# Stages two and three of a three-layer kernel in token groups of 460 and 464 columns; last stores, two sums and first keys issued from other engines

## The chip, the cores and the metric

The kernel runs on one core of one Trainium2 chip. A time is the device time of one execution in microseconds (us). Before the change it was 1575.15 us, the median of three runs (1574.21 to 1580.14).

## The reference, cut to what matters

```python
def _attn_ref(q, k, v):                       # 8 batches, 8 heads, 576 positions, 64 wide
    q_s = softmax(q, axis=-1)                 # over the 64 of a head
    k_s = softmax(k, axis=2)                  # over the 576 positions
    kv = np.einsum('bhsd,bhse->bhde', k_s, v)
    return np.einsum('bhsd,bhde->bhse', q_s, kv)

x = attn_out.transpose(0, 2, 1, 3).reshape(4608, 512)
g = np.maximum(x @ w_in1, 0.0) ** 2           # 512 -> 2048
y = g @ w_out1                                # 2048 -> 512
h = y @ w_in2                                 # 512 -> 2048
out = (h / (1 + np.exp(-h))) @ w_out2         # 2048 -> 512, fp32 result of 4608 x 512
```

## The kernel before, in words

There are four stages. Stage one computes the attention for nine blocks of 512 tokens (`i` from 0 to 8) and, for each block, `x @ w_in1` with relu and square. Its matmuls write `h`, ScalarE turns them into the tile `gs`, and for each of eight channel pairs `j` four sums of quarters follow: two on VectorE (`g_first`), two on GpSimd (`g_second`). Then GpSimd issues the store of seven pieces to the DRAM tensor `g1d` (`g_store`).

The three later matmuls, `@ w_out1` (stage two, `ph == 1` in the code), `@ w_in2` with silu (stage three, `ph == 2`) and `@ w_out2` (last stage, `ph == 3`), each use a two by two scheme with seven products in place of eight. Tokens are split in two halves, so 2304 columns stand for 4608 tokens. Each stage takes these columns in five groups `u`, of 448, 448, 448, 448 and 512. A group has 56 steps, a step six matmuls: two output or input halves times three, since each fp32 operand is split in a rounded part (`ah`, `wh`) and a rest (`al`, `wl`) and the product rest by rest is left out. So one group of one stage is 336 matmuls, every one with a weight tile of its own of 128 columns.

For each step SP loads a piece of 128 rows by the group's columns into `al` (14 steps ahead), ScalarE copies it rounded to `ah`, and VectorE subtracts to leave the rest in `al` (six steps ahead). Results come out of the PSUM banks `x`, `d` and `a` into slots of the tile `st`, and GpSimd issues their stores to `x2d` (after stage two) and `g2d` (after stage three). The last stage transposes on VectorE (`turn`) and stores to `out` (`store`); for the last group the stores are shared out over GpSimd, SP and ScalarE, 16 for each half of the result. While a stage runs, the weights of the next are made ready: sums `wt` on GpSimd, splits `wB`, `wT`, `wN` on ScalarE and VectorE. From block 1 on each engine executes in the order in which the code is written; only the first block is ordered by a scheduler. DMAs issued from SP and ScalarE share eight completion semaphores in turn, so each waits until the one eight before it has landed. In the first block `r_load` loads the last 64 positions of the keys, `kr`, with GpSimd as the issuing engine.

Of the kernel before, what the change touches and what calls it, by code (L numbers as in the profile page):

```python
# [8 lines left out]
F32 = mybir.dt.float32  # L9
# [4 lines left out]
ALU = mybir.AluOpType  # L14
# [11 lines left out]
def kernel(  # L26
# [56 lines left out]
    P = 128  # L83
# [5 lines left out]
    HB = TB // 2  # L89
    NB = NT // TB  # L90
    KC = DM // P
    NF = DFF // P
    NG = NF // 2
# [40 lines left out]
    def back(*ts):  # L134
# [8 lines left out]

    GROUPS = NB * HB // (2 * Q)
    NS = -(-NB // 2)
    sizes = [GROUPS // NS + (u >= NS - GROUPS % NS) for u in range(NS)]
    starts = [sum(sizes[:u]) * 2 * Q for u in range(NS + 1)]
    x2d = [dpool.tile([P, 7, NB * HB], F32, name=f"x2d{e}") for e in range(2)]
    g2d = [
        [dpool.tile([P, 7, n * 2 * Q], F32, name=f"g2d{u}_{j}") for j in range(NG)]  # L150
        for u, n in enumerate(sizes)
    ]
    g1d = [dpool.tile([P, 7, NB * HB], F32, name=f"g1d{j}") for j in range(NG)]
    wd = {(ph, f): dpool.tile([P, DM], F32, name=f"wd{ph}_{f}") for ph in (1, 2, 3) for f in range(NF)}

# [589 lines left out]

    def g_second(i, j):
        t = g_place(i, j)
        gp.tensor_tensor(t[:, S2], t[:, S1], t[:, A11], op=ALU.subtract)
        gp.tensor_tensor(t[:, S4], t[:, A12], t[:, S2], op=ALU.subtract)

    def g_store(i, j):
        o = slice(A21, 7) if i == 0 else slice(0, A21 + 1) if i is None else slice(0, 7)
# [73 lines left out]
    steps += [(3, u, n, j, u == ORDER3[-1]) for u in ORDER3 for n, j in SUMMED]  # L826
    xs = {}

    def width(u):
        return sizes[u] * 2 * Q  # L830

    def a_load(ph, u, n, c):

        lo = room(F32R, "al")
        slot = PRODUCTS[n][0]
        w = width(u)
        cols = slice(starts[u], starts[u + 1])
        if ph == 1:
            src = g1d[c][:, slot, cols]
        else:  # L840
            src = x2d[c][:, slot, cols] if ph == 2 else g2d[u][c][:, slot]
        sp.dma_start(out=f32(lo)[:, 0:w], in_=src)
        xs[ph, u, n, c] = [None, lo]

    def a_split(ph, u, n, c):
        hi = room(F32R, "ah")
        lo = xs[ph, u, n, c][1]
        o = slice(0, width(u))
        ac.copy(hi[:, o], f32(lo)[:, o])
        ve.tensor_tensor(lo[:, o], f32(lo)[:, o], f32(hi)[:, o], op=ALU.subtract)  # L850
        xs[ph, u, n, c][0] = hi
# [22 lines left out]

    def step(ph, u, n, j, done):
        name, begins = INTO[n]
        w = width(u)
        now = due()
        if ph == 2:
            k = j % 2  # L880
            if begins:
                ps[name, k] = bank(name)
            for c in range(2):
                hi, lo = xs[ph, u, n, c]
                mm3(
                    ps[name, k][:, 0:w], begins and c == 0, c == 1, W[ph, j, n],
                    slice(c * P, (c + 1) * P), hi[:, 0:w], lo[:, 0:w], not begins,
                )
                if j == NG - 1:
                    back(hi, lo)  # L890
                    del xs[ph, u, n, c]
            for fn in now:
                fn()
            hidden_after(ph, u, n, k, j)
        else:
            hi, lo = xs.pop((ph, u, n, j))
            for e in range(2):
                if begins and j == 0:
                    ps[name, e] = bank(name)
                mm3(  # L900
                    ps[name, e][:, 0:w], begins and j == 0, j == NG - 1, W[ph, j, n],
                    slice(e * P, (e + 1) * P), hi[:, 0:w], lo[:, 0:w], not begins,
                )
            back(hi, lo)
            for fn in now:
                fn()
            if j == NG - 1:
                for e in range(2):
                    if ph == 1:
                        hidden_after(ph, u, n, e, e)  # L910
                    else:
                        out_after(u, n, e, done)
        if done:
            back(W.pop((ph, j, n)))
# [2 lines left out]

    def hidden_after(ph, u, n, k, j):

        w = width(u)  # L920
        to = g2d[u][j] if ph == 2 else x2d[j][:, :, starts[u]:starts[u + 1]]

        def silu(x):
            if ph == 2:
                ac.activation(x, x, AF.Silu)
        p = ps[INTO[n][0], k][:, 0:w]
        h = keep.setdefault(k, {})

        def new(*names):
            for x in names:  # L930
                h[x] = slots.popleft()

        def store(*which):
            for s, x in which:
                gp.dma_start(out=to[:, s], in_=h[x][:, 0:w])
                slots.append(h.pop(x))

        at_ = lambda x: h[x][:, 0:w]

        if n == 0:  # L940
            new("c11")
            ac.copy(at_("c11"), p)
        elif n == 2:
            new("c12")
            ac.copy(at_("c12"), p)
        elif n == 4:
            ve.tensor_tensor(at_("c11"), p, at_("c11"), op=ALU.add)
            back(ps.pop(("a", k)))
        elif n == 1:
            new("c22")  # L950
            ac.copy(at_("c22"), p)
            d = ps["d", k][:, 0:w]

            def then():
                ve.tensor_tensor(at_("c22"), d, at_("c22"), op=ALU.add)
                later(lambda: silu(at_("c22")), 2)
            later(then)
        elif n == 5:
            new("c21", "s1", "s2")
            if ph == 2:  # L960
                ac.activation(at_("c21"), p, AF.Silu)
            else:
                ac.copy(at_("c21"), p)
            back(ps.pop(("x", k)))
            silu(at_("c11"))

            def then():
                ve.tensor_tensor(at_("s1"), at_("c21"), at_("c22"), op=ALU.add)
                ve.tensor_tensor(at_("c21"), at_("c11"), at_("c21"), op=ALU.subtract)
                ve.tensor_tensor(at_("s2"), at_("s1"), at_("c11"), op=ALU.subtract)  # L970
                store((A22, "c22"), (S1, "s1"), (S3, "c21"), (A11, "c11"))
            later(then)
        elif n == 6:
            ve.tensor_tensor(at_("c12"), p, at_("c12"), op=ALU.add)
            back(ps.pop(("d", k)))
            mine = keep.pop(k)

            def then():
                a12, s2 = (mine[x][:, 0:w] for x in ("c12", "s2"))
                silu(a12)  # L980

                def last():
                    s4 = slots.popleft()
                    ve.tensor_tensor(s4[:, 0:w], a12, s2, op=ALU.subtract)
                    for s, t in ((S2, mine["s2"]), (A12, mine["c12"]), (S4, s4)):
                        gp.dma_start(out=to[:, s], in_=t[:, 0:w])
                        slots.append(t)
                later(last)
            later(then, 3)

    def out_after(u, n, e, done):

        w = width(u)
        p = ps[INTO[n][0], e][:, 0:w]
        p0, u2, u3 = (st[e][:, s, 0:w] for s in (4, 5, 6))
        if n == 0:
            ac.copy(p0, p)
        elif n == 2:
            ac.copy(u2, p)
        elif n == 4:  # L1000
            ve.tensor_tensor(p0, p, p0, op=ALU.add)
            back(ps.pop(("a", e)))
            turn(u, 1, e, p0)
        elif n == 1:
            ac.copy(u3, p)
            d = ps["d", e][:, 0:w]

            def then():
                ve.tensor_tensor(u3, d, u3, op=ALU.add)
                turn(u, 0, 2 + e, u3)  # L1010
            later(then)
        elif n == 6:
            ve.tensor_tensor(u2, p, u2, op=ALU.add)
            back(ps.pop(("d", e)))
            turn(u, 1, 2 + e, u2)
            if e == 1:
                store(u, 1, done)
        elif n == 5:
            turn(u, 0, e, p)
            back(ps.pop(("x", e)))  # L1020
            if e == 1:
                store(u, 0, done)

    def turn(u, half, e, x):

        w = width(u)
        t = st[half][:, 0:4].rearrange("p n c -> p (n c)")[:, 0:4 * w]
        ve.transpose(
            t.rearrange("p (b e i) -> p e b i", e=4, i=Q)[:, e],
            x.rearrange("p (b i) -> p b i", i=Q),  # L1030
        )

    def store(u, half, ends):
        w = width(u)
        t = st[half][:, 0:4].rearrange("p n c -> p (n c)")[:, 0:4 * w]
        n = 2 * Q
        for i in range(NB):
            m0, m1 = (max(0, min(w, i * HB + x - starts[u])) // n for x in (0, HB))
            if m0 == m1:
# [15 lines left out]
            for j, nj, o in os:  # L1055
                for a in range(P // Q):
                    for r in range(2):
                        (gp if not ends or (a, r) in ((0, 0), (2, 1)) else ac if r else sp).dma_start(
                            out=o[a, half, r],
                            in_=t[a * Q + j:a * Q + j + nj].rearrange(  # L1060
                                "j (m r f) -> r j m f", r=2, f=P
# [25 lines left out]

    warm = [spool.tile([P, 1], F32, name=f"warm{x}") for x in range(3)]
    kv_load(0, 0, ac)
    r_load(0, 0, gp, ac)  # L1090
    ve.memset(warm[0], 0.0)
    ve.memset(warm[2], 0.0)
    gp.partition_all_reduce(warm[1], warm[0], P, bass_isa.ReduceOp.max)
# [187 lines left out]
```

## Time and profile before

| | us |
|---|---|
| median of three runs | 1575.15 |
| profiled execution, device time | 1569.96 |
| its span, first to last instruction | 1568.1 |
| TensorE busy in it | 1527.3 (97%) |
| VectorE, ScalarE, GpSimd busy | 1125.8, 907.0, 625.2 |

In the profile PE is TensorE's matmul, PEld its weight load, DVE VectorE, ACT ScalarE, POOL GpSimd, SP the engine that only issues DMAs; a q behind a name is that engine's sequencer, which issues DMAs and handles semaphores. All instructions of the kernel's body pass through one helper and have line L73, so they are told apart by the names of their tiles. Stage one lasts until about 500 us, stage two to 854, stage three to 1204, the last stage to 1554. A busy PE is not yet a PE at its peak.

### The profile page before, as it was taken

The numbers are of one execution on the slowest core, as the hardware profiler recorded it, in microseconds if no ns is written. First come the engines' busy times: TensorE is split into PE (matmuls) and PEld (weight loads), VectorE is DVE, ScalarE is ACT, GpSimd is POOL, SyncE is SP. The second block draws the span as 40 slices with busy tenths as digits, with TensorE's granted clock in tenths as the row PEclk, the third lists the DMA queues.
The fourth block names the chain that finished last, engine by engine and source line by source line (L and its number), as shares of the span: only waits on it lengthen the run. The fifth ranks groups of instructions, "written<-read, shape, count | busy, mean of one in ns | idle before, by whom it ended". The sixth has DMA issues, their size and how long they took to land.

```text
span 1568.1 us, 25313 instructions
## 1 busy us (share of the span) xinstructions
PE 1527.3 (97%) x7679; PEld 1329.8 (85%) x7679; DVE 1125.8 (72%) x2263; ACT 907.0 (58%) x1927; POOL 625.2 (40%) x966
## 2 busy tenths in 40 slices
PE   5899999999999999999999999999999999999996
PEld 3678888888888899999988999999888899889995
DVE  7887888986627977767888776767757865564644
ACT  7876666666545755554575664555646744454431
POOL 1035556655659020211144544445485040605231
PEclk9999999999999999999999999999999999999998
DMA  8969999999977898989996776877889777868761
GB/s 216 287 204 286 310 326 312 328 328 298 333 242 240 292 309 271 331 274 328 304 318 224 245 285 245 297 272 261 310 290 315 235 237 200 247 182 240 207 228 47
DMA packets 270376, 419.58 MB, mean 268 GB/s; under 512 B 70272, under 2 KB 202496, under 8 KB 270240
## 3 DMA queue, kind: packets, MB, share of 16 engines
q1 hardware_dynamic: 216912, 246.39, 51.9%
q0 software_dynamic: 50976, 170.50, 30.0%
q10 hardware_dynamic: 2352, 1.08, 0.3%
q8 instruction: 60, 0.98, 0.3%
q14 instruction: 76, 0.62, 0.1%
HBM read 236.72 MB, written 181.14 MB: 266 GB/s over the span
## 4 chain that ended last, share of the span: by engine, by line
PE 91%; DVE 3%; DMA 2%; ACT 2%; issue 1%; POOL 1%; SPq 0%; POOLq 0%; ACTq 0%; DVEq 0%
PE x L73 37%; PE h L73 23%; PE d L73 19%; PE a L73 9%; PE kvps L73 2%; PE xps L73 2%; DVE wu L73 1%; ACT gs L73 0%; DMA al<-g2d 0%; DMA kr<-in_k_dram 0%; DMA wraw<-in_moe_w_in_dram 0%; DVE al L73 0%; DVE xr L73 0%; DMA g1d<-gs 0%; DMA g2d<-st 0%
## 5 line engine op out<-in xcount | busy, mean ns | idle before, releaser
L73 DVE TENSOR_TENSOR al<-al,ah 128x448 fp32r<-128x448 f32 (+1 forms) x630 | 374.6, 644 | 181.4 <-ACT ah L73 179.2
L73 ACT CAST ah<-al 128x448 fp32r<-128x448 f32 (+1 forms) x630 | 334.6, 577 | 143.6 <-PE x L73 54.1
L73 PE MATMUL h<-x,wh 128*128 128x512 f32 x1152 | 364.3, 396 | 1.3 <-ACT wh L73 0.7
L73 PE MATMUL x<-ah,wT 128*128 128x448 f32 (+1 forms) x960 | 287.3, 370 | 0.0
L73 PEld LDWEIGHTS h<-x,wh 128*128 128x128 f32 x1152 | 214.5, 189 | 47.2 <-ACT wh L73 1.2
L73 ACT COPY st<-x 128x448 f32<-128x448 f32 (+1 forms) x181 | 98.1, 543 | 248.5 <-PE x L73 237.2
L73 PE MATMUL h<-x,wl 128*128 128x512 f32 x576 | 225.9, 392 | 0.0
L73 PEld LDWEIGHTS x<-ah,wT 128*128 128x128 f32 x960 | 180.3, 188 | 19.8 <-ACT st L73 0.7
L73 POOL DMA_DIRECT2D out_dram<-st x184 | 96.6, 535 | 243.5 <-DVE st L73 237.0
L73 POOL DMA_DIRECT2D g2d<-st x262 | 140.8, 542 | 130.4 <-ACT st L73 64.1
L73 PE MATMUL x<-al,wT 128*128 128x448 f32 (+1 forms) x480 | 177.6, 370 | 0.0
L73 POOL TENSOR_TENSOR gs<-gs 128x256 f32<-128x256 f32 x144 | 124.2, 865 | 106.4 <-DVE gs L73 50.9
L73 ACT ACTIVATE gs<-h 128x512 f32<-128x512 f32 x144 | 86.0, 597 | 136.6 <-PE h L73 129.3
L73 PE MATMUL a<-ah,wB 128*128 128x448 f32 (+1 forms) x480 | 148.4, 370 | 0.0
L73 PE MATMUL x<-ah,wB 128*128 128x448 f32 (+1 forms) x480 | 144.7, 373 | 0.0
L73 PE MATMUL d<-ah,wB 128*128 128x448 f32 (+1 forms) x480 | 143.6, 370 | 0.0
L73 PE MATMUL d<-ah,wT 128*128 128x448 f32 (+1 forms) x480 | 143.5, 370 | 0.0
L73 PE MATMUL x<-ah,wN 128*128 128x448 f32 (+1 forms) x480 | 143.5, 370 | 0.0
L73 PEld LDWEIGHTS h<-x,wl 128*128 128x128 f32 x576 | 108.6, 189 | 23.6 <-issue 0.5
L73 DVE TENSOR_TENSOR st<-st 128x448 f32<-128x448 f32 (+1 forms) x161 | 100.0, 647 | 25.9 <-ACT st L73 21.0
L73 DVE TENSOR_TENSOR gs<-gs 128x256 f32<-128x256 f32 x144 | 74.9, 525 | 41.3 <-ACT gs L73 24.0
L73 PEld LDWEIGHTS x<-ah,wB 128*128 128x128 f32 x480 | 90.9, 189 | 9.7
(130 smaller groups left out, 2689.5 us busy)
## 6 DMA issues: line engine op xcount, KB each, us to landing
g1d<-gs POOLq DMA_DIRECT2D x64, 896.0 KB, 6.6
al<-g1d SPq DMA_DIRECT2D x224, 224.0 KB, 4.2
al<-g2d SPq DMA_DIRECT2D x224, 224.0 KB, 3.3
g2d<-st POOLq DMA_DIRECT2D x210, 224.0 KB, 3.7
al<-g1d SPq DMA_DIRECT2D x56, 256.0 KB, 4.2
al<-g2d SPq DMA_DIRECT2D x56, 256.0 KB, 3.1
g2d<-st POOLq DMA_DIRECT2D x52, 256.0 KB, 3.7
al<-x2d SPq DMA_DIRECT2D x56, 224.0 KB, 5.1
```

Of the source, the lines that this page charges most:

```text
L73: got = fn(*a, **kw)
```

## The change

Stages two and three take their 2304 columns in groups of 460, 460, 460, 460 and 464; the last stage keeps 448 and 512. Since the groups of stage three and of the last stage no longer agree, `g2d` becomes one tensor per `j` over all columns, as `g1d` and `x2d` already are. For the last block of stage one `g_second` is issued on VectorE in place of GpSimd. The 16 stores of each half of the last group are issued on SP and ScalarE alone, eight each. The first block's `kr` is loaded from SP in place of GpSimd, as SP's first two DMAs.

```diff
-    sizes = [GROUPS // NS + (u >= NS - GROUPS % NS) for u in range(NS)]
-    starts = [sum(sizes[:u]) * 2 * Q for u in range(NS + 1)]
+    sizes = [(GROUPS // NS + (u >= NS - GROUPS % NS)) * 2 * Q for u in range(NS)]
+    even = [NB * HB // NS // 4 * 4] * (NS - 1)
+    even.append(NB * HB - sum(even))
+    SIZES = {1: even, 2: even, 3: sizes}
+    STARTS = {ph: [sum(x[:u]) for u in range(NS + 1)] for ph, x in SIZES.items()}
-    g2d = [
-        [dpool.tile([P, 7, n * 2 * Q], F32, name=f"g2d{u}_{j}") for j in range(NG)]
-        for u, n in enumerate(sizes)
-    ]
+    g2d = [dpool.tile([P, 7, NB * HB], F32, name=f"g2d{j}") for j in range(NG)]
...
     def g_second(i, j):
         t = g_place(i, j)
-        gp.tensor_tensor(t[:, S2], t[:, S1], t[:, A11], op=ALU.subtract)
-        gp.tensor_tensor(t[:, S4], t[:, A12], t[:, S2], op=ALU.subtract)
+        by = ve if i == NB - 1 else gp
+        by.tensor_tensor(t[:, S2], t[:, S1], t[:, A11], op=ALU.subtract)
+        by.tensor_tensor(t[:, S4], t[:, A12], t[:, S2], op=ALU.subtract)
...
-                        (gp if not ends or (a, r) in ((0, 0), (2, 1)) else ac if r else sp).dma_start(
+                        (gp if not ends else ac if r else sp).dma_start(
...
-    r_load(0, 0, gp, ac)
+    r_load(0, 0, sp, ac)
```

Two places where instructions move. The first is the end of stage one. On GpSimd before the change, the sums `gs` stand between the stores of `g1d` for j = 1 to 4:

```order
L73 DMA g1d1_128<-gs_186 896x1x256
L73 TENSOR_TENSOR gs_187<-gs_187 128x256 x2
L73 DMA g1d2_129<-gs_187 896x1x256
L73 TENSOR_TENSOR gs_187<-gs_187 128x256 x2
L73 DMA g1d3_130<-gs_187 896x1x256
L73 TENSOR_TENSOR gs_188<-gs_188 128x256 x2
L73 DMA g1d4_131<-gs_188 896x1x256
```

GpSimd after the change, from the last weight sums `wt` to the store of j = 6:

```order
L73 TENSOR_TENSOR wt_5181<-wB21_5174,wt_5181 128x256
L73 TENSOR_TENSOR wt_5190<-wB21_5183,wt_5190 128x256
L73 DMA g1d1_96<-gs_154 896x1x256
L73 DMA g1d2_97<-gs_155 896x1x256
L73 DMA g1d3_98<-gs_155 896x1x256
L73 DMA g1d4_99<-gs_156 896x1x256
L73 DMA g1d5_100<-gs_156 896x1x256
L73 DMA g1d6_101<-gs_154 896x1x256
```

Only stores are left there. VectorE in the same place before the change, from two splits `wB` of weights to the splits `wT` for the second product (`al` is a split of stage two's first group):

```order
L73 TENSOR_TENSOR wB11_5214<-wB11_5214 128x256
L73 TENSOR_TENSOR gs_187<-gs_187 128x256 x2
L73 TENSOR_TENSOR gs_188<-gs_188 128x256 x4
L73 TENSOR_TENSOR al_5352<-al_5352,ah_5440 128x448
L73 TENSOR_TENSOR al_5354<-al_5354,ah_5445 128x448
L73 TENSOR_TENSOR al_5373<-al_5373,ah_5467 128x448
L73 TENSOR_TENSOR al_5375<-al_5375,ah_5472 128x448
L73 TENSOR_TENSOR gs_186<-gs_186 128x256 x2
L73 TENSOR_TENSOR al_5395<-al_5395,ah_5495 128x448
L73 TENSOR_TENSOR al_5397<-al_5397,ah_5500 128x448
```

VectorE after the change, the same stretch:

```order
L73 TENSOR_TENSOR wB11_5182<-wB11_5182 128x256
L73 TENSOR_TENSOR gs_155<-gs_155 128x256 x6
L73 TENSOR_TENSOR gs_156<-gs_156 128x256 x6
L73 TENSOR_TENSOR al_5320<-al_5320,ah_5408 128x460
L73 TENSOR_TENSOR al_5322<-al_5322,ah_5413 128x460
L73 TENSOR_TENSOR gs_156<-gs_156 128x256 x2
L73 TENSOR_TENSOR al_5341<-al_5341,ah_5435 128x460
L73 TENSOR_TENSOR al_5343<-al_5343,ah_5440 128x460
L73 TENSOR_TENSOR gs_154<-gs_154 128x256 x2
L73 TENSOR_TENSOR al_5363<-al_5363,ah_5463 128x460
L73 TENSOR_TENSOR al_5365<-al_5365,ah_5468 128x460
```

There are 16 sums `gs` in place of 8 in this stretch; the splits keep their order. The second place is the end of the program on ScalarE, before the change: the stores of one half of the last group, the last two splits, the stores of the other half.

```order
L73 CAST ah_16167<-al_16085 128x448
L73 DMA out_0_dram<-st_5530 32x3x128 x3
L73 DMA out_0_dram<-st_5530 32x4x128 x3
L73 CAST ah_16196<-al_16100 128x448
L73 CAST ah_16205<-al_16111 128x448
L73 DMA out_0_dram<-st_5529 32x3x128 x3
L73 DMA out_0_dram<-st_5529 32x4x128 x3
```

The same on ScalarE after the change:

```order
L73 CAST ah_16135<-al_16053 128x448
L73 DMA out_0_dram<-st_5498 32x3x128 x4
L73 DMA out_0_dram<-st_5498 32x4x128 x4
L73 CAST ah_16164<-al_16068 128x448
L73 CAST ah_16173<-al_16079 128x448
L73 DMA out_0_dram<-st_5497 32x3x128 x4
L73 DMA out_0_dram<-st_5497 32x4x128 x4
```

Eight stores stand where six stood, ahead of the last two splits too. SP changes in the same way, and GpSimd's last instruction becomes a store of the group before the last.

## Rows read from the trace of the kernel before

**Rows 1.** Busy time by stretch (us; then PE, PEld, DVE, ACT, POOL; clock, DMA share, GB/s).
```profile
512.00:515.00 3.00, 3.00 (x9) 2.63 (x8) 3.00 (x9) 2.22 (x7) 0.90 (x1) 0.50 0.97 300
642.00:710.00 68.00, 68.00 (x337) 63.02 (x336) 51.12 (x107) 36.32 (x77) 10.62 (x21) 1.00 0.91 305
778.00:854.00 76.00, 76.00 (x337) 62.92 (x336) 66.75 (x113) 50.55 (x107) 31.96 (x34) 1.00 0.87 292
1128.00:1204.00 76.00, 76.00 (x337) 62.92 (x336) 48.34 (x77) 40.17 (x80) 54.26 (x90) 1.00 0.88 308
1204.00:1220.00 16.00, 15.14 (x73) 12.84 (x72) 15.96 (x36) 13.89 (x38) 6.92 (x13) 1.00 0.88 313
```

**Rows 2.** Chain that ended last: start us, us, what; a 448 and a 512 group.
```profile
525.21 9.72 PE x L73 x48
789.03 10.88 PE d L73 x48
```

**Rows 3.** Groups of instructions by form: busy us, mean ns of one, idle before.
```profile
L73 PEld LDWEIGHTS x<-ah,wT 128*128 128x128 f32 x960 | 180.3, 188 | 19.8 <-ACT st L73 0.7
L73 DVE TENSOR_TENSOR al<-al,ah 128x448 fp32r<-128x448 f32 x504 | 291.9, 627 | 149.3 <-ACT ah L73 147.9 <-DMA al<-g2d 1.2
```

**Rows 4.** Timeline (start us, us, what), TensorE in a 448 and a 512 group (loads, a matmul).
```profile
620.10 0.39 PEld L73 LDWEIGHTS a<-ah,wB 128*128 128x128 f32 x2
620.30 0.57 PE L73 MATMUL a<-ah,wB 128*128 128x448 f32 x2
...
799.98 0.41 PEld L73 LDWEIGHTS x<-ah,wT 128*128 128x128 f32 x2
```

**Rows 5.** Timeline of TensorE at half clock: two matmuls, two others between them.
```profile
513.53 0.57 PE L73 MATMUL x<-al,wB 128*128 128x448 f32 x1
...
514.65 0.57 PE L73 MATMUL x<-al,wB 128*128 128x448 f32 x1
```

**Rows 6.** Timeline around the end of stage one, five engines.
```profile
452.88 0.89 DVE L73 TENSOR_TENSOR gs<-gs 128x256 f32<-128x256 f32 x2 [2.88 <-ACT gs L73]
...
468.95 14.04 POOL L73 TENSOR_TENSOR wt<-wB,wt 128x256 f32<-128x256 f32 x18
...
487.34 3.90 DVE L73 TENSOR_TENSOR wB<-wB 128x256 fp32r<-128x256 f32 x2 [11.22 <-POOL wt L73]
...
495.21 1.78 POOL L73 TENSOR_TENSOR gs<-gs 128x256 f32<-128x256 f32 x2
...
503.17 0.63 ACT L73 ACTIVATE gs<-gs 128x512 f32<-128x512 f32 x1
...
509.58 1.78 DVE L73 TENSOR_TENSOR al<-al,ah 128x448 fp32r<-128x448 f32 x1
...
511.42 0.47 PE L73 MATMUL x<-al,wB 128*128 128x448 f32 x1 [3.53 <-DVE al L73]
```

**Rows 7.** Closing line L1276, engine op xcount: ns min/median/max, first and last start.
```profile
L1276 POOLq EVENT_SEMAPHORE  x4: 17/17/17, 1567.4 to 1568.0; - x4
L1276 POOLq DRAIN  x3: 46/102/10698, 1556.7 to 1567.9; - x3
```

**Rows 8.** Timeline of the last 20 us, issues of stores and ScalarE's last splits.
```profile
1549.76 1.03 ACT L73 CAST ah<-al 128x448 fp32r<-128x448 f32 x2 [13.59 <-DMA out_dram<-st]
1555.03 3.12 ACTq L73 DMA_DIRECT2D out_dram<-st  x6
...
1555.29 2.18 POOL L73 DMA_DIRECT2D out_dram<-st  x4 [6.30 <-DVE st L73]
```

**Rows 9.** DMA issues after 1554 us: xcount, KB each, median us to landing.
```profile
out_dram<-st SPq DMA_DIRECT2D x3, 64.0 KB, 3.2
out_dram<-st ACTq DMA_DIRECT2D x3, 48.0 KB, 2.4
```

**Rows 10.** Timeline of the first 10 us: the first keys `kr` and their user.
```profile
1.28 1.38 POOL L73 DMA_DIRECT2D kr<-in_k_dram  x2 [0.83 <-POOLq L1264]
...
9.12 0.29 DVE L73 TENSOR_TENSOR m<-m,kr 128x128 f32<-128x128 f32 x1 [0.77 <-DMA kr<-in_k_dram]
```

More of the change, by code (lines that the diff above doesn't have):

```diff
@@ L827, with width, columns @@
     xs = {}
-    def width(u):
-        return sizes[u] * 2 * Q
+    def width(ph, u):
+        return SIZES[ph][u]
+    def columns(ph, u):
+        return slice(*STARTS[ph][u:u + 2])
     def a_load(ph, u, n, c):
@@ L835, in a_load @@
         slot = PRODUCTS[n][0]
[L836 to L841, printed above, removed]
+        w = width(ph, u)
+        src = (g1d, x2d, g2d)[ph - 1][c][:, slot, columns(ph, u)]
         sp.dma_start(out=f32(lo)[:, 0:w], in_=src)
@@ L847, in a_split @@
         lo = xs[ph, u, n, c][1]
-        o = slice(0, width(u))
+        o = slice(0, width(ph, u))
         ac.copy(hi[:, o], f32(lo)[:, o])
@@ L876, in step @@
         name, begins = INTO[n]
-        w = width(u)
+        w = width(ph, u)
         now = due()
@@ L918, in hidden_after @@
     def hidden_after(ph, u, n, k, j):
-        w = width(u)
-        to = g2d[u][j] if ph == 2 else x2d[j][:, :, starts[u]:starts[u + 1]]
+        w = width(ph, u)
+        to = (g2d if ph == 2 else x2d)[j][:, :, columns(ph, u)]
         def silu(x):
@@ L991, in out_after @@
     def out_after(u, n, e, done):
-        w = width(u)
+        w = width(3, u)
         p = ps[INTO[n][0], e][:, 0:w]
@@ L1024, in turn @@
     def turn(u, half, e, x):
-        w = width(u)
+        w = width(3, u)
         t = st[half][:, 0:4].rearrange("p n c -> p (n c)")[:, 0:4 * w]
@@ L1033, in store @@
     def store(u, half, ends):
-        w = width(u)
+        w = width(3, u)
         t = st[half][:, 0:4].rearrange("p n c -> p (n c)")[:, 0:4 * w]
-        n = 2 * Q
+        n, starts = 2 * Q, STARTS[3]
         for i in range(NB):
```

## The prediction

> **What bounds the kernel now.** I read the busy table first: TensorE is busy 1527.3 us of the 1568.1 us span, so a gain is either fewer ns per matmul or one of the few gaps. Then the busy time by stretch, to see where a gap is. Stages two, three and last show TensorE busy all the time; only 0.86 us is missing, at the start of the last stage, where VectorE is busy 15.96 of 16 us [rows 1]. DMA is at 0.91 in stage two, VectorE at 88% and GpSimd at 71% in the last groups of stages two and three [rows 1]: other engines are close, not late.
>
> Next, what one matmul costs. The chain gives 9.72 us for 48 matmuls of 448 columns, 202.5 to 202.7 ns each, and 10.88 us for 48 of 512, 226.7 ns [rows 2]. Columns grew by 14.3%, time by 11.9%: something is not paid per column at 448. The groups by form and the timeline say what it may be. A weight load takes 188 ns whatever the group [rows 3]. At 448, two loads span 0.39 us: the second starts 0.20 us after the first, and the second matmul can't start before that load is over, which leaves some 14 ns between. At 512 two loads span 0.41 us, so the loads stand 0.22 apart with some 38 ns idle between them [rows 4]. So I read 202.6 as bound by the weight load (188 plus a hand-over) and 226.7 as bound by columns. At half clock two matmuls of 448 start 1.12 us apart with two between, 373 ns each, which is 448 columns at 1.2 GHz and nothing more [rows 5].
>
> Then the gaps, by the timeline. At the end of stage one TensorE waits 3.53 us at 511.42 for a split `al` on VectorE, and the granted clock is 0.50 for some 3 us behind it [rows 1, 6]. VectorE is late because it stood 11.22 us behind GpSimd, which had 18 sums `wt` in one piece, 14.04 us, and its sums `gs` besides [rows 6]. Last, the end: TensorE stops at 1554.3, and the span ends at 1568.1. GpSimd's drain begins at 1556.65, as its last store is issued, lasts 10.70 us to 1567.35, and the closing barrier comes behind it [rows 7].
>
> **The change part by part.**
>
> *Group widths.* A group is 336 matmuls. Before, a stage is 336 x (4 x 202.6 + 226.7) = 348.5 us. For 460 columns the trace shows nothing; I take the 512 row as clock time plus a fixed part: 512 / 2.4 = 213.3, so 13.4 ns over it. Then 460 is 191.7 + 13.4 = 205.0 ns and 464 is 206.7, both above the load's 202.6. After: 336 x (4 x 205.0 + 206.7) = 345.0 us, 3.5 less; for two stages -7.1 us. Bounds: if time between 448 and 512 is a straight line (207.1 and 208.6), nothing is gained; if all of the 226.7 is per column (203.7 and 205.4), -11.4; the weight load as floor everywhere gives -16.3. I take -7.1, near the middle.
>
> The Trainium skill (TensorE: Matmul & The Clock Gate, Back-to-back issue gap) speaks against this edit: it gives columns / 2.4 + 2.5 ns for isolated matmuls at full clock, so by it 2304 columns in five groups cost the same however they are cut, 0 us. It also gives a load of 128 columns as 128 / 1.2, 107 ns. The trace shows 202.6 and 226.7 where the rule has 189 and 216, and a load of 188 ns, so the measurement decides; the rule stands as a rival below.
>
> Other engines get the same columns, so their busy time stays. Rows of 460 columns are 1840 bytes at multiples of 1840, not of 256. No row shows what that costs a DMA. Below: nothing. Above: with the DMA share at 0.91 in stage two [rows 1], transfers 10% longer still fit; beyond, TensorE waits. I take 0, covered by loads issued 14 steps ahead (some 17 us), and price the excess as a rival.
>
> The last group of stage three shrinks from 76.2 to 69.4 us (336 x 206.7), while the weight sums and loads for the last stage stay as they are: GpSimd's 54.3 us and DMA at 0.88 of 76 us, 67 us [rows 1]. The start of the last stage already lacks 0.86 us. Bounds 0 and the whole 6.8 us; I take +1.5. In stage two VectorE has 66.8 of 76 us there, some 4 of which shrink with the columns, so 62 of 69.4: still covered, 0.
>
> *Sums moved at the end of stage one.* GpSimd loses 16 sums, 0.89 us each by the row that shows two in 1.78; VectorE gets 16 at 0.445 (two in 0.89 with GpSimd quiet) [rows 6], 7.1 us. What waits for them are the stores of `g1d`, which free the `gs` tiles. Does VectorE reach the late split sooner? Its 23 instructions from 487.34 to the end of that split (2 `wB`, 10 `gs`, 7 `al`, 4 `wT`) are 6 x 0.445 + 10 x 0.445 + 7 x 0.627 [rows 3] = 11.5 us by quiet durations, but took 24.0, with GpSimd's sums running beside. Now there are 12 sums more, +5.3: 16.8 us. GpSimd releases VectorE two sums earlier, at about 485.6, so it arrives at 502.4, or some 505 with the remaining weight sums of GpSimd beside it. The last pair waits for ScalarE's last square at 503.8 [rows 6]: four sums and a split later is 506.2. TensorE needs it at 507.9. So the stall goes: -3.5, and with it the slow clock: nine matmuls at 373 instead of 203, -1.5. What is late next is VectorE itself, 1.7 us ahead of TensorE with two weight splits and an `al` per step, 1.2 us against a step of 1.23. Bounds: -5.1 and +1.5 (if VectorE's seven extra us all fall behind). I take -5.1.
>
> *Last stores.* Without its last stores GpSimd's drain comes some 45 us earlier, beside TensorE's work. Then the end is the last landing, plus SP's semaphores and the barrier, together about 1 us (0.7 of it behind the drain [rows 7]). Issues: six took 3.12 us on ScalarE, 0.52 each [rows 8], so eight take 4.16, and the eighth must wait for the fourth of its queue: issued 1556.5, landed 2.4 later, 1558.9; issued by 1559.3 it lands 3.2 after its start [rows 9], 1562.1. End at 1563.1 instead of 1568.1: -5.0. The two issues more on ScalarE in the half before stand ahead of the last two splits, which began at 1549.76 behind them [rows 8]; 1.0 us later the first `al` is there near 1552, about when TensorE, six steps on, comes to it: +0.2, at most +0.6. Bounds of this part: -6.0 and, if the drain waits at the end all the same, +0.6. I take -4.8.
>
> *First keys.* `kr` issued at 1.28 on GpSimd is waited for by VectorE, 0.77 us until 9.1 [rows 10]. From SP it starts half a us sooner, but SP's loads behind it move two issues, 0.9 us, later. Bounds -1.9 (start of that chain by the scheduler's new order) and +0.9. I take the wait, -0.8.
>
> Sum: -7.1 + 1.5 - 5.1 - 4.8 - 0.8 = -16.3. Against the profiled execution, 1569.96, that is 1553.7; that execution was 5.2 us below the median of the runs, and I put the same step on the median: 1575.15 - 16.3 = 1558.9, so 1559.
>
> **The rivals.**
> - *Time is linear in columns* (the fixed part is not a load's floor). For: only two widths are seen, and two points fit any line. Against: loads follow each other without a pause at 448 and with 38 ns at 512. Then -7.1 falls away: 1566. The Trainium skill's rule above ends here too.
> - *All of the excess is per column*: 1559 - 4.3 = 1555. For: it fits the same rows.
> - *The stall at the end of stage one moves* to VectorE, which now has the sums. For: VectorE was busy nearly without a pause there. Against: half of that was inflated. The 5.1 stays: 1564.
> - *The drain stays at the end.* For: no row shows a drain without stores before it at the end. Against: it starts as GpSimd's own last issue is taken. 1575.15 - 11.5 + 0.6 = 1564.
> - *Slower: rows off 256 bytes make DMA the bound of stage two.* Place: loads of `g1d` and stores of `x2d`, 511 to 854. It decides from 10% longer transfers; at 20%, 0.91 x 1.2 = 1.09 stretches 343 us by 31, while stage two's 3.5 is lost: 1559 + 31 + 3.5 = 1593. For: 0.91. Against: loads have a lead of 17 us, and `x2d`'s bytes are few.
>
> By the Trainium skill (DMA: Bandwidth & Descriptors, How a descriptor splits into AXI transactions) a row that doesn't start at 256 bytes fetches from the boundary below. From its counts, 1792 bytes are 56 beats and rows of 1840 at these offsets 58 to 64; that estimate is 5 to 6% more, a share of 0.96, and no stall. No run here shows it.
>
> **How the numbers follow.** No change from measurement is told below about 0.5%, 7.9 us, so "faster" is below 1567.3. Chances: forecast 0.50 (own range 1553 to 1565, from the bounds at the last stage's start, the end and the first keys), linear 0.15 (half of it still over 7.9 us), all per column 0.13, moved stall 0.10, drain stays 0.06, slower 0.06. Faster: 0.49 + 0.07 + 0.13 + 0.08 + 0.05 = 0.82. Slower 0.05. The rest, 0.13, is the same. The range 1548 to 1571 leaves out the slow rival and the far ends of two gains added.
>
> **What would show it.** In the profile after: 48 matmuls of 460 in 9.84 us (9.94 if linear, 9.78 if per column); no wait of over 1 us by TensorE and no granted clock of 0.50 near 510 us; GpSimd's long drain beginning near 1500 us and the span ending about 9 us behind the last matmul in place of 14; VectorE's wait for `kr` gone; less than 3 us missing at the start of the last stage. I am wrong if 48 matmuls take 9.94 us or more, or if loads of `al` end waits of TensorE in stage two.

## The result

The changed kernel takes 1559.55 us, the median of six runs (1556.43 to 1562.24); the kernel before, on the same chip, 1578.99 (1574.21 to 1580.14). The ratio is 0.9885, with a 95% interval of 0.9865 to 0.9904. On a second chip it was 0.9932 (0.9916 to 0.9948). The profiled execution takes 1559.24 us with a span of 1557.4; that of before had 1569.96 and 1568.1. So the two profiles differ by 10.7 us, where the medians differ by 19.4 on the first chip and 11.8 on the second. Both the 10.7 and what is over it have to be explained.

### The profile page after: what moved, and what is told of

It is laid out like the page before. It is cut to its first block, busy times and chain, and to the rows that moved or that the text cites. A ratio compares the mean times of both kernels' runs of the same rounds, so it can differ in the third digit from the quotient of the medians.

```text
span 1557.4 us, 25290 instructions
## 1 busy us (share of the span) xinstructions
PE 1527.5 (98%) x7679; PEld 1328.5 (85%) x7679; DVE 1125.5 (72%) x2279; ACT 905.2 (58%) x1927; POOL 606.6 (39%) x940
## 4 chain that ended last, share of the span: by engine, by line
PE 94%; DMA 2%; ACT 2%; DVE 1%; issue 1%; POOL 0%; SPq 0%; ACTq 0%; POOLq 0%; DVEq 0%
PE x L73 37%; PE h L73 24%; PE d L73 19%; PE a L73 10%; PE kvps L73 2%; PE xps L73 2%; DMA g1d<-gs 1%; ACT q L73 0%; DMA wraw<-in_moe_w_in_dram 0%; PE qps L73 0%; DMA q<-in_q_dram 0%; DMA g2d<-st 0%; DVE xr L73 0%; DMA xr<-qd 0%; DMA qd<-q 0%
## 5 line engine op out<-in xcount | busy, mean ns | idle before, releaser
L73 DVE TENSOR_TENSOR al<-al,ah 128x460 fp32r<-128x460 f32 (+3 forms) x630 | 371.8, 640 | 184.7 <-ACT ah L73 183.6
L73 ACT CAST ah<-al 128x460 fp32r<-128x460 f32 (+3 forms) x630 | 334.8, 577 | 145.3 <-PE x L73 52.6
L73 PE MATMUL x<-ah,wT 128*128 128x460 f32 (+3 forms) x960 | 286.8, 369 | 0.0
L73 PE MATMUL x<-al,wT 128*128 128x460 f32 (+3 forms) x480 | 177.2, 369 | 0.0
L73 PE MATMUL a<-ah,wB 128*128 128x460 f32 (+3 forms) x480 | 148.2, 369 | 0.0
L73 PE MATMUL d<-ah,wT 128*128 128x460 f32 (+3 forms) x480 | 143.4, 370 | 0.0
L73 PE MATMUL x<-ah,wB 128*128 128x460 f32 (+3 forms) x480 | 143.3, 369 | 0.0
L73 PE MATMUL d<-ah,wB 128*128 128x460 f32 (+3 forms) x480 | 143.3, 369 | 0.0
L73 PE MATMUL x<-ah,wN 128*128 128x460 f32 (+3 forms) x480 | 143.3, 369 | 0.0
L73 DVE TENSOR_TENSOR st<-st 128x460 f32<-128x460 f32 (+1 forms) x161 | 101.1, 654 | 25.7 <-ACT st L73 22.0
```

Source lines behind the costliest of these rows:

```text
L73: got = fn(*a, **kw)
```

## The profile after

Busy time by stretch, changed kernel, columns as in [rows 1]; the first line is the stretch in which TensorE stood still before.

```profile
506.00:512.00 6.00, 5.87 (x29) 4.98 (x28) 3.56 (x9) 2.35 (x7) 0.82 (x1) 1.00 1.03 373
...
642.00:710.00 68.00, 68.00 (x331) 61.76 (x330) 50.62 (x105) 36.56 (x75) 10.72 (x20) 1.00 0.92 305
778.00:854.00 76.00, 76.00 (x364) 67.90 (x363) 66.46 (x120) 51.03 (x115) 34.96 (x39) 1.00 0.88 290
1128.00:1204.00 76.00, 76.00 (x366) 68.48 (x365) 51.71 (x86) 42.23 (x92) 57.69 (x96) 1.00 0.89 312
1204.00:1220.00 16.00, 15.13 (x71) 12.39 (x70) 16.00 (x40) 14.61 (x40) 3.56 (x7) 1.00 0.68 237
```

The reader is to see three things. The clock is 1.00 at the end of stage one and 0.13 us are missing there, where [rows 1, 6] had 0.50 and a wait of 3.53 us. The DMA share went from 0.91 to 0.92 in stage two and nothing waits. The start of the last stage lacks 0.87 us, as before.

The chain, which lists a group's matmuls in pieces of 48 or 12 (start us, us, what): stage two at 460, at 464, then two pieces of 460 in stage three.

```profile
521.04 9.92 PE x L73 x48
...
789.03 10.08 PE d L73 x48
...
896.98 2.51 PE x L73 x12
...
984.66 2.48 PE x L73 x12
```

460 columns take 9.92 / 48 = 206.7 ns in stage two and 206.7 or 209 in stage three; 464 take 210, or 209 in stage three. By these, stage two is 336 x (4 x 206.7 + 210.0) = 348.4 us without its waits, and was 348.5. The widths gave nothing against [rows 2].

The timeline around the end of stage one, VectorE and GpSimd, answers to [rows 6].

```profile
486.58 5.43 DVE L73 TENSOR_TENSOR wB<-wB 128x256 fp32r<-128x256 f32 x2 [7.30 <-POOL wt L73]
491.93 4.85 DVE L73 TENSOR_TENSOR gs<-gs 128x256 f32<-128x256 f32 x12
...
502.91 2.48 DVE L73 TENSOR_TENSOR gs<-gs 128x256 f32<-128x256 f32 x6
505.30 0.63 DVE L73 TENSOR_TENSOR al<-al,ah 128x460 fp32r<-128x460 f32 x1
```

Twelve sums take 4.85 us, 0.40 each: with GpSimd's sums gone they run at their quiet rate. The split behind the last sums ends at 505.93, where the late one of before ended at 511.36.

What TensorE's missing 0.13 us hangs on now is in the chain of waits:

```profile
499.20 10.30 DMA g1d<-gs
...
509.65 0.58 ACT ah L73
...
510.26 0.65 DVE al L73
...
510.95 1.11 PE d L73 x4
```

A store of `g1d`, issued at 499.20, lands at 509.50; ScalarE waits 4.9 us for that, then comes its copy `ah`, then VectorE's split, then TensorE. So VectorE is no longer the late one, and there is no slack left behind this store.

The closing line, then the stores after 1545 us (count, KB each, median us to landing); they answer to [rows 7, 9].

```profile
L1276 POOLq EVENT_SEMAPHORE  x4: 17/17/17, 1556.7 to 1557.3; - x4
L1276 POOLq DRAIN  x3: 46/102/9742, 1501.2 to 1557.2; - x3
```

```profile
out_dram<-st ACTq DMA_DIRECT2D x6, 64.0 KB, 2.3
out_dram<-st SPq DMA_DIRECT2D x5, 64.0 KB, 2.3
```

A drain of 9.74 us is still there, but it begins at 1501.2, beside TensorE's work. The last matmul ends at 1549.5 and the span 7.9 us later, in place of 13.8.

At the head, VectorE gets the first keys 2.5 us sooner than in [rows 10], though it still waits for them, 1.44 us in place of 0.77. The chain of waits shows where the early start goes. Changed kernel:

```profile
6.64 0.29 DVE L73 TENSOR_TENSOR m<-m,kr 128x128 f32<-128x128 f32 x1 [1.44 <-DMA kr<-in_k_dram]
```

```profile
71.52 5.45 DMA wraw<-in_moe_w_in_dram
...
103.92 1.16 PE h L73 x5
```

The kernel before, same chain:

```profile
70.11 5.95 DMA wraw<-in_moe_w_in_dram
...
103.67 1.38 PE h L73 x6
```

At 70 us both wait for a weight load `wraw`, and the row of `h` that runs on stands at 103.92 after and 103.67 before. Nothing of the early start is left.

So the 10.7 us between the profiles are: 5.1 from the start of stage two to the last matmul (1054.1 us before, 1049.0 after), 5.9 behind the last matmul, and 0.3 lost at the head. My theory at this point: the widths are worth about 0 and the other 8.7 us of the first chip's medians come from the kernel before, whose runs vary. The rivals were a longer stall, a longer drain or a longer head in its timed runs.

## Experiments: one part at a time

Each of four kernels has one part of the change alone; the others are put back, by these lines (changed kernel on the plus side). The new layout of `g2d`, one tensor per `j`, stays in all four, and no kernel has it alone; so each row below is that part and the layout together.

```diff
-    SIZES = {1: sizes, 2: sizes, 3: sizes}      # widths back
+    SIZES = {1: even, 2: even, 3: sizes}
-        by = gp                                 # sums back
+        by = ve if i == NB - 1 else gp
-  (gp if not ends or (a, r) in ((0, 0), (2, 1)) else ac if r else sp).dma_start(   # stores back
+  (gp if not ends else ac if r else sp).dma_start(
-    r_load(0, 0, gp, ac)                        # keys back
+    r_load(0, 0, sp, ac)
```

> Only the group widths of stages two and three are changed (460 x4 and 464). The prediction's theory (one part of a matmul is a floor of 202.6 ns at 448, above it clock time plus 13.4 ns): 7 us less than before. The theory from the trace of the changed kernel (206.7 ns at 460, 210 at 464, so 336 x (4 x 206.7 + 210.0) = 348.4 us a stage as before): 0, within 2 us either way, and the stall and the half clock near 510 us as before.

> Only the two sums of stage one's last block are moved from GpSimd to VectorE. Prediction's theory: 5 us less than before, no wait of TensorE over 1 us and no granted clock of 0.50 near 510 us. Rival (the stall moves to VectorE): within 1 us of before. If the timed runs of the kernel before carry a longer stall there than its profiled run, 8 us or more less.

> Only the last group's stores are moved from GpSimd to SP and ScalarE. Prediction's theory: 5 us less than before; by the trace of the changed kernel (the span ends 7.9 us behind the last matmul in place of 13.8) 6 us. If the timed runs of the kernel before carry a longer drain than its profiled run, 9 us or more less. Rival (the drain waits at the end all the same): 0 to 0.6 more.

> Only the first block's last keys are loaded from SP in place of GpSimd. Prediction's theory: 0.8 us less than before. Theory from the trace of the changed kernel (its stage one ends at the same distance from the span's start, 0.3 us later): 0, within 1 us. If the head is what makes the timed runs of the kernel before longer than its profiled run: 4 us or more less.

All four against the same 35 runs of before (median 1573.74, 1567.62 to 1581.20), 12 runs each:

| alone | median us | ratio, 95% interval | us |
|---|---|---|---|
| widths | 1572.59 | 0.9980 (0.9963 to 0.9997) | -3.1 (-5.8 to -0.5) |
| sums | 1567.22 | 0.9962 (0.9946 to 0.9979) | -6.0 (-8.5 to -3.3) |
| stores | 1567.66 | 0.9957 (0.9940 to 0.9974) | -6.8 (-9.4 to -4.1) |
| keys | 1574.97 | 1.0007 (0.9989 to 1.0025) | +1.1 (-1.7 to +3.9) |

Sums and stores each do what was predicted, alone; the stores do somewhat more. With the sums alone the first 93 us of stage two take 4.9 us less (88.05 in place of 92.91 to the same matmul), and the stretch of the stall, whose clock in before was 0.81, reads, in before and then with the sums alone:

```profile
508.00:517.00 9.00, 5.58 (x20) 5.03 (x21) 8.97 (x18) 4.22 (x12) 4.40 (x6) 0.81 0.98 327
```

```profile
508.00:517.00 9.00, 8.83 (x44) 7.53 (x43) 8.48 (x21) 9.00 (x25) 0.00 (x0) 1.00 1.00 310
```

With the stores alone the long drain begins at 1513.7, and the span ends 7.5 us behind the last matmul:

```profile
L1276 POOLq DRAIN  x3: 51/93/9850, 1513.7 to 1570.1; - x3
```

The keys alone are worth nothing that can be measured, and neither is the layout of `g2d`, unless the two cancel. The profile of that kernel is the interesting one: its span is 1577.5 us, 9.4 over that of before, though it differs from it only by the issue of two loads and that layout. Its stretch around the stall, and its chain at 448 columns in stage two:

```profile
508.00:517.00 9.00, 4.92 (x15) 4.12 (x14) 8.97 (x16) 3.87 (x11) 5.57 (x7) 0.69 0.95 322
```

```profile
527.59 9.92 PE x L73 x48
```

48 matmuls of 448 take 9.92 us here, 206.7 ns each, and do so through the first four groups of stage two; in [rows 2] they take 9.72. That is 336 x 4 x 4.0 ns = 5.4 us. The first two groups of its last stage run the same way but for their first 96 matmuls, 2.3 us more. The stores alone show the same in both places; the sums alone have 206.7 in the last stage and 202.6 in stage two, the widths alone 206.7 in the last stage, the one in which they still have 448. So 448 columns have two spacings, and a run keeps one of them for a long stretch. Whether before itself does was asked last, of the unchanged kernel:

> The kernel before, unchanged, to see whether it is itself that varies. Theory of two spacings: 48 matmuls of 448 take 9.72 or 9.92 us through a whole stretch, and the profiled time follows: near 1570 us if 9.72 everywhere, 2.7 us more for the first two groups of the last stage at 9.92, 5.4 us more for stage two. Rival (the chip or the head varies): 9.72 everywhere and a time that differs all the same. Against itself its ratio is 1 within 0.003.

It took 1573.18 us (ratio to itself 0.9993, 0.9972 to 1.0014), the profiled execution 1573.43 with a span of 1571.6, 3.5 over the first profile. Its chain in stage two and in the last stage:

```profile
526.17 9.73 PE x L73 x48
...
1226.32 9.92 PE x L73 x48
```

and the first profile of before at that last place:

```profile
1225.22 9.73 PE x L73 x48
```

The last stage's first half is at 206.7 ns in the one and 202.6 in the other; 2.3 of the 3.5 us come in there, and 1.3 at the end of stage one, where the matmul behind the stall starts 4.4 us after the one ahead of it in place of 3.9, and half clock lasts longer. So the kernel before varies by itself, in the two ways seen here, and its first profile was a run with the short spacing in all of stage two and the last stage, and with the shortest stall of the five seen. A long spacing in both stages and a longer stall, 5.4 + 2.3 + 1.3, add up to 9.0 us, the distance from that profile to the first chip's median. That its timed runs were slow for just this is not shown, since only a profiled execution tells the spacing. In the other sets of runs here the kernel before has medians of 1571.35 to 1576.17 us; the first chip's 1578.99 is the highest, so the ratio of 0.9885 flatters the change, and 0.9932 is nearer to what the profiles show.

## Experiments: the widths

> The changed kernel with groups of 448 and 512 in stages two and three again. Theory of two spacings: matmuls of 448 run a whole stage either at 202.7 or at 206.7 ns (the trace of one kernel showed the one, two others the other), matmuls of 460 always at 206.7; so the best runs equal those of the changed kernel, others are 5 or 11 us longer, and runs spread by more than the changed kernel's 6 us; the median is 0 to 6 us above it. The prediction's theory: 7 us above the changed kernel. Linear theory: equal to it.

> The changed kernel once more, on the same chip as the one without its widths, as their common measure. 48 matmuls of 460 take 9.92 us again whatever happened at the stage's start; the median is 15 to 20 us under before.

The first is the changed kernel with the widths line above put back; the second is the changed kernel itself. Without the widths: 1558.31 us, 0.9924 (0.9904 to 0.9944); four of its six runs lie at 1557.6 to 1558.6, the others at 1562.7 and 1566.4. With them: 1560.72 us, 0.9932 (0.9916 to 0.9948), 1559.4 to 1563.3. The widths are worth nothing that can be measured once the stall is gone: the intervals overlap, and the best runs are 1.8 us better without. The outliers without them, 4 and 8 us up, are of the size of a stage at 206.7 ns (5.4 us), or of that and half of the last stage; that they were just that is not shown, since the profiled run (span 1555.8) had the short spacing in both.

Then the law itself, by other widths. Each of the three kernels was executed once (1566.43, 1561.46 and 1561.71 us), so they are read for the spacing of their matmuls and not for their times:

```diff
-    SIZES = {1: even, 2: even, 3: sizes}
+    SIZES = {1: [384, 448, 448, 512, 512], 2: [432, 456, 464, 472, 480], 3: sizes}   # map 1
+    SIZES = {1: [464, 464, 464, 448, 464], 2: [460, 464, 452, 468, 460], 3: sizes}   # map 3
+    SIZES = {1: [400, 416, 496, 480, 512], 2: [512, 496, 488, 408, 400], 3: sizes}   # map 4
```

> Other group widths: stage two 384, 448, 448, 512, 512, stage three 432, 456, 464, 472, 480. Prediction's theory (floor by the weight load, above it clock time plus 13.4 ns): 202.6 ns at 384, 432 and 448, then 203.4 at 456, 206.7 at 464, 210.1 at 472, 213.4 at 480. Linear theory (0.377 ns per column): 178.5 at 384, 196.6 at 432, 205.7 at 456, 208.7 at 464, 211.7 at 472, 214.7 at 480. Theory of two spacings: up to 448 either 202.7 or 206.7, from 456 on 206.7 at least.

> Other group widths: stage two 464, 464, 464, 448, 464, stage three 460, 464, 452, 468, 460. Prediction's theory: 206.7 ns at 464, 203.4 floored by 202.6 at 452, 208.4 at 468. Linear theory: 208.7 at 464, 204.2 at 452, 210.2 at 468. If 464 alone has an unlucky rhythm (matmuls 205 and 215 ns apart in turn), 210 at 464 in every place, and the 448 group behind it shows which of 202.7 and 206.7 follows.

> Other group widths once more: stage two 400, 416, 496, 480, 512, stage three 512, 496, 488, 408, 400. Theory from the map: columns at 2.4 GHz plus 13.3 ns up to where a matmul would start before the load that began with the one before it is over, some 190 ns: 180.0 at 400, 183.3 at 408, 186.7 at 416. Above: 216.7 at 488 and 220.0 at 496 if the excess has gone there, up to 3.3 more if it hasn't. Linear theory: 184.6 at 400, 190.6 at 416, 217.7 at 488, 220.7 at 496.

Chain of map 1 in stage two, at 384, 448 and 512 columns:

```profile
521.50 8.32 PE x L73 x48
...
597.81 9.92 PE x L73 x48
...
723.78 10.88 PE x L73 x48
```

Map 3, at 464 and at 448:

```profile
535.36 10.03 PE x L73 x48
...
744.87 9.73 PE x L73 x48
```

Map 4, at 400, 416, 496 and 480:

```profile
518.89 8.64 PE x L73 x48
...
580.00 8.96 PE x L73 x48
...
646.24 10.72 PE x L73 x48
...
720.64 10.40 PE x L73 x48
```

Divided by 48 (in stage three by 12), against columns / 2.4 + 13.3 ns, all in ns:

| columns | line | measured | | columns | line | measured |
|---|---|---|---|---|---|---|
| 384 | 173.3 | 173.3 | | 460 | 205.0 | 206.7, 209 |
| 400 | 180.0 | 180.0 | | 464 | 206.7 | 209, 210 |
| 408 | 183.3 | 185 | | 468 | 208.3 | 212 |
| 416 | 186.7 | 186.7 | | 472 | 210.0 | 213 |
| 432 | 193.3 | 196 | | 480 | 213.3 | 216.7 |
| 448 | 200.0 | 202.6, 206.7 | | 488 | 216.7 | 220 |
| 452 | 201.7 | 207 | | 496 | 220.0 | 220, 223.3 |
| 456 | 203.3 | 209 | | 512 | 226.7 | 226.7 |

The base is a straight line: from 384 to 512 columns a matmul grows by 53.4 ns, 0.417 a column, which is one column per cycle at the granted 2.4 GHz, and 13.3 ns stand on top. Up to 416 columns, and at 512, a matmul takes that (at 408 1.7 more). Between 432 and 496 it takes up to 7 ns more, and not always the same. All theories fall in part. The straight line through 448 and 512 would put 384 at 178.5. The floor by the weight load is gone altogether, and the timeline of map 1 at 384 says why (loads, then matmuls):

```profile
530.35 0.36 PEld L73 LDWEIGHTS a<-ah,wB 128*128 128x128 f32 x2
...
530.35 0.33 PE L73 MATMUL a<-al,wB 128*128 128x384 f32 x1
```

Two loads span 0.36 us, so the second begins 0.17 after the first; each is recorded with 188 ns. They overlap: 188 ns is how long a load takes until it is done, not how often one can begin. In these kernels nearly every load begins 2 to 4 ns after a matmul has begun, at all widths, and ends about 190 ns after it. By the line, the next matmul is due 3 to 30 ns after that end at the widths from 432 to 496, those with an excess, and 37 ns after it at 512, which has none; 408, with its 1.7 ns, doesn't fit this. That the two are cause and effect is not shown; no run changed the one without the other. What picks one of two spacings at 448 is open as well: 448 behind groups of 384 ran at 206.7, behind groups of 464 at 202.6. Of the profiled kernels with four groups of 448 in stage two, the two without the stall had 202.6, and of the four with it two had 206.7; but map 1 had 206.7 though TensorE waited no more than 1.2 us. In the last stage the pattern is another: all seven profiled kernels that have sums, stores and keys changed and 448 columns there run its first two groups at 202.6 behind their first 96 matmuls, and five of the six others at 206.7. Which part does it is not shown.

The Trainium skill (TensorE: Matmul & The Clock Gate, Back-to-back issue gap) has columns / 2.4 + 2.5 ns for isolated matmuls at full clock. The slope agrees with these runs; the fixed part here is 13.3 ns, each matmul with a weight tile of its own. Its consequence, that five groups cost the same however they are cut, holds among 384, 400, 416 and 512 only.

So a better cut avoids the middle:

```diff
-    SIZES = {1: even, 2: even, 3: sizes}
+    SIZES = {1: [512, 384, 512, 384, 512], 2: [512, 384, 512, 384, 512], 3: sizes}
     # and in the second kernel also, for the last stage:
+    sizes = [512, 512, 512, 384, 384]
+    ORDER3 = [0, 1, 4, 2, 3]
```

> The changed kernel with stages two and three in groups of 512, 384, 512, 384, 512. Theory from the map of widths (time is columns at 2.4 GHz plus 13.3 ns at 384 and 512, and between 432 and 480 a further 2 to 7 ns): 336 x (3 x 226.7 + 2 x 173.3) = 345.0 us a stage, so 3.4 and 4.6 us less than the changed kernel's stages, 8 us in all, 1552. If a step of 384 (1.04 us) leaves VectorE, ScalarE or the DMA queues late, waits of TensorE on al or ah in those groups, and as long as or longer than the changed kernel. Prediction's theory (no matmul under 202.6): 336 x 2 x 29.3 = 20 us a stage longer than that, slower than before.

> The same, and the last stage too, in groups of 512, 512, 384, 512, 384 in the order they run. Theory from the map: another 3.5 us less (345.0 in place of 348.5 us), 1548, and no half or whole stage at 206.7 ns left, so a spread of the runs under 6 us. Rival (other engines late at 384, or the stores of the last stage): no better than with stages two and three alone.

Stages two and three alone: 1553.76 us, ratio 0.9877 (0.9856 to 0.9898). All three: 1549.41 us (1549.25 to 1550.33), ratio 0.9852 (0.9831 to 0.9872), the fastest kernel here, 10 to 11 us under the changed kernel's medians on two other chips (0.9852 of before against 0.9885 and 0.9932). Between the profiles of the two new kernels lie 4.2 us: 2.8 come in the last stage, 1.7 ahead of stage two, where both have the same code. For the kernel with all three, a 384 and a 512 group of its last stage in the chain, and its second 384 group of stage two by stretch:

```profile
1458.34 10.88 PE d L73 x48
...
1496.76 8.32 PE x L73 x48
```

```profile
710.00:760.00 50.00, 50.00 (x290) 50.00 (x289) 38.74 (x88) 27.61 (x64) 5.93 (x11) 1.00 0.94 317
```

DMA is at 0.94 and VectorE at 77% there, and TensorE waits for neither. In stage three it does wait: twice, in the groups of 384, 0.5 us for ScalarE to empty a PSUM bank into `st`, and once 0.7 us for a copy `ah`. That stage takes 347.7 us from its first matmul to that of the last stage, where stage two takes 345.1.

```profile
969.12 0.44 PE L73 MATMUL x<-ah,wT 128*128 128x384 f32 x1 [0.52 <-ACT st L73]
```

The four runs lie within 1.1 us of each other, and the five with stages two and three alone within 1.7, where the changed kernel's lie within 5.8 and 3.9. As far as these nine runs tell, most of the spread goes with the widths of stages two and three; that it is the second spacing which goes is likely, but no run shows it.

## Why the prediction came out as it did

The time, 1559.0 forecast and 1559.55 measured, is nearer than its parts, and that is luck. The sums and stores were right, the widths were not: the profiles show -10.7 us where the parts were to give -16.3. What made up for it is that I laid the 5.2 us between the profile of before and its median on the changed kernel too, whose median lies 0.3 over its profile. The linear rival had the nearer sum, -9.2, and missed the time, 1566, for that same reason.

- *Group widths, -7.1.* This step failed. I read two widths as a floor by the weight load (448) and clock time plus 13.4 ns (512). The second half was right, 13.3 at 384, 400 and 416 too; the first was wrong, and 460 and 464 do not lie on the line but 2 to 4 ns above it: 206.7 to 209 and 209 to 210 where 205.0 and 206.7 were taken. Measured: -0.4 against the short spacing, by the two profiles. Against a run of before with 206.7 ns at 448 in stage two it is some 5 more, which may be why the widths alone came out at -3.1. Of the signs I named, 9.92 us for 48 is what the straight line gives (9.94), so this rival had the size right here; as a law it is refuted at 384. I had the hint in hand: in the trace of before, 202.5 to 202.7 is a mean of single distances of 199, 203 and 207 ns from start to start, and a floor is steady.
- *Start of the last stage, +1.5.* 0: 0.87 us are missing as before, with GpSimd at 57.7 of 76 us in the stretch ahead of it.
- *Sums, -5.1.* Right in mechanism and size: -4.9 in the profile of the sums alone, -6.0 timed. No wait over 1 us, no clock of 0.50. The split behind the sums was forecast to end at 506.2 and ends at 505.93. The stall did not move to VectorE, since the sums run at 0.40 us in the absence of GpSimd's. What I had as late next, VectorE, was wrong: it is the store of `g1d` that ScalarE waits for, and it costs some 0.3 us: the matmul at 510.95 starts 0.51 us after the one ahead of it, where 0.21 is usual.
- *Last stores, -4.8.* Right in mechanism: the drain begins as GpSimd's last store is issued. Gain 5.9, since the stores landed 2.3 us after issue where I took 2.4 and 3.2.
- *First keys, -0.8.* The wait was to be gone and is not: it comes 2.5 us sooner and is 1.44 us long. That early start is lost again, since a load at 70 us ends the chain there all the same: 0.3 lost in the profile, +1.1 (-1.7 to +3.9) timed. The step that failed is that a wait at the head was taken to set the time.
- *Rows off 256 bytes.* No wait on a load of `al` in stage two. By the Trainium skill (DMA: Bandwidth & Descriptors, How a descriptor splits into AXI transactions) I had estimated a share of 0.96; it is 0.92 against 0.91, so the measurement decides for next to nothing.
- *From profile to median.* I put the step of the profile on the median as it stood. That the runs of before differ by 0.6% was in the numbers (1569.96 profiled, 1574 to 1580 timed), and I asked neither why nor whether the change would end it.

## What to carry to other kernels

Two widths do not make a law: before cutting a stage into other group sizes, measure the time of a matmul at the widths in question and their neighbours, and take the cut that lies on the line, here 384 and 512 in place of five nearly equal groups. Look at the single distances, not at their mean, and at whether a run keeps one of two rhythms; a kernel whose profile is faster than all its timed runs is telling that. A duration in the trace is a latency until two of them are seen not to overlap.

## What the runs showed of the hardware that was not expected

- Weight loads of 188 ns each follow one another every 173.3 ns at 384 columns.
- Matmuls of 448 columns run for whole stretches either at 202.6 or at 206.7 ns, which moves this kernel by 2.3 us in the first two groups of the last stage and by 5.4 in four groups of stage two.
- GpSimd's drain behind its last store takes 8.9 to 10.7 us in the fourteen traces, at the end of the program or some 50 us ahead of it.
